# A retention layer and a snake MLP on one core: the second projection of blocks 1 to 8 as seven products of quarters, in a new order of all steps

## The chip, the cores and the metric

The kernel runs on one core of a Trainium2 chip. The metric is device time in microseconds (us), the median of several runs. Five engines work side by side, each through its own queue of instructions in order: TensorE (PE in the profile; its loads of weights are PEld), VectorE (DVE), ScalarE (ACT), GpSimd (POOL) and SyncE (SP, which issues DMAs here). Semaphores order them. PE writes its products to PSUM, which has 8 banks of 512 float32 per partition; GpSimd doesn't read PSUM in this kernel.

## The reference

A retention layer (attention with a decay in place of a softmax) for 8 batches of 576 positions and 8 heads of 64, and behind it an MLP with a snake activation, on 4608 tokens of 512 features:

```python
scores = scale * np.matmul(q, k.transpose(0, 1, 3, 2))
Dmat = np.where(rel >= 0, gamma[:, None, None] ** rel[None, :, :], 0.0)   # rel = pos[:, None] - pos[None, :]
attn_out = np.matmul(scores * Dmat[None, :, :, :], v)                      # per batch and head
x = attn_out.transpose(0, 2, 1, 3).reshape(4608, 512)
h = x @ w_in                                                               # 512 -> 2048
s = np.sin(alpha * h)
g = h + s * s / (alpha + 1e-09)
out = g @ w_out                                                            # 2048 -> 512
```

## The kernel before

The tokens fall into 9 blocks of 512: blocks 0 to 7 are the first 512 positions of a batch each, block 8 the last 64 positions of all eight. The program is one long table, `STEPS`: the order of the entries is the order in which the steps are issued, and with it the order on each engine; a letter behind a colon names the engine of a step (A ScalarE, V VectorE, G GpSimd, P TensorE, S SyncE), and `name=number` puts a tile into a numbered buffer or bank. A loop at the end of the kernel calls one function for each entry. Nothing else sets the order, and semaphores follow from who writes and reads which tile.

Attention of a batch `b`, in two halves `p` of 256 positions:

- `LD` loads raw q, k, v (SyncE), `CA` scales them to float16, `TU` and `TK` (PE and a copy) or `XP` (a DMA) turn q and k.
- `OU` makes the states k^T v of four chunks on PE; `TS` or `EV` copies them, `MA`, `MB` (or `NS`) and `ST` run the decay from chunk to chunk.
- `SC` makes the scores on PE, `MK` masks them on VectorE, `VA`, `VB` and `SA` add up values and states, and `KP` copies the result to the block's input `x`. `RL` is a mark that waits for `VA`, on GpSimd or another engine, or a drain of PE.
- Names with `E` (`LE`, `CE`, `XE`, `ESC` to `EKP`) do the same for the last 64 positions of the batches, block 8.

The MLP of block `n`, in 16 units `u` of 128 hidden features:

- `PR` (line 757) is the first projection of a unit: four products of 512 tokens into a bank; a few units go in two halves of 256 columns.
- `SI` (765) takes the sine on ScalarE, `SQ` (775, 776) squares it on ScalarE, VectorE or GpSimd, and `PD` (780) adds: g = sq * inva + h, on VectorE, and frees the bank.
- `G2.n.c.part` (796) is the second projection: for each of four chunks `c` of 128 tokens, 16 products of 512 output columns, in four parts; `FI` copies the bank to SBUF, `OS` (806, 807) stores it with two DMAs. The products of block n stand among the `PR` of block n + 1.

`KB` issues products of zeros on PE while it has nothing else to do. `WI` and `WO` load the two weights on GpSimd's queue, cast to float16. The file already has functions for a second projection by quarters (`TT`, `SM`, `PP`, `CP`, `AD`, `OQ`, lines 813 to 888); the table of before doesn't call them.

Of the kernel before, what the change touches and what calls it, by code (L numbers as in the profile page):

```python
# [23 lines left out]
CN; AR; EY; MC; Z0; ZE; FS; LD.0.k.0 raw.0.k.0=0; LD.0.q.0 raw.0.q.0=1; LD.0.v.0 raw.0.v.0=2; LD.0.q.1 raw.0.q.1=3  # L24
LD.0.k.1 raw.0.k.1=4; CA.0.k.0.0:G k16.0.0=0; LD.0.v.1 raw.0.v.1=5; CA.0.q.0.1:V q16.0.0=1; CA.0.k.0.1:V; CA.0.q.0.0:V
CA.0.v.0.2:A v16.0.0=2; LD.1.q.1 raw.1.q.1=6; KB.16.256.6; KB.44.64.6; OU.0.0 kv.0.0.0=0 kv.0.0.1=1
TU.0.k.0.0 tr.0.k.0=2; LD.1.q.0 raw.1.q.0=7; CA.0.q.1.2:G q16.0.1=3; TU.0.k.0.1; TU.0.q.0.0 tr.0.q.0=3
TK.0.k.0.0:V kT.0.0=4; TU.0.q.0.1; TS.0.0:V kvs.0=8; TK.0.k.0.1:A; CA.0.k.1.2:V k16.0.1=5; LD.1.v.0 raw.1.v.0=9
TK.0.q.0.2:A qT.0.0=6; WI.0; TU.0.q.1.2 tr.0.q.1=0; WI.2; TS.0.1:V; SC.0.0.1 sc.0.0.1=4; CA.0.v.1.2:V v16.0.1=7
TU.0.k.1.2 tr.0.k.1=1; LD.1.k.0 raw.1.k.0=10; MA.0.1:G s32.0.1=8; SC.0.0.0 sc.0.0.0=6; TK.0.k.1.2:A kT.0.1=9; MB.0.1:G  # L30
AT al=2; WI.1; ST.0.1:V s16.0=10; LD.1.k.1 raw.1.k.1=11; AC:A; TK.0.q.1.2:A qT.0.1=11; ST.0.0:V
CA.1.q.1.2:G q16.1.1=12 <ST.0.0; KB.10.256.3; OU.0.1 kv.0.1.0=0 kv.0.1.1=1; MA.0.2:G s32.0.2=13; TS.0.2:A
MK.0.0.1 ret.0.0.1=14; MB.0.2:G; WI.3; MK.0.0.0 ret.0.0.0=15; SC.0.1.0 sc.0.1.0=2; ST.0.2:G; TU.1.q.1.2 tr.1.q.1=0
WO.0; MK.0.1.0 ret.0.1.0=16; TK.1.q.1.2:A qT.1.1=17; SC.0.1.1 sc.0.1.1=4; LD.1.v.1 raw.1.v.1=12
CA.1.q.0.2:G q16.1.0=18; MK.0.1.1 ret.0.1.1=19; VA.0.0 o.0.0=6; RL.0.0:P; VB.0.0; SA.0.0; VA.0.1 o.0.1=2
KP.0.0.2:V x.0=13; RL.0.1:P; VB.0.1; SA.0.1; PR.0.2.0 hps.0.2=0; KP.0.1.0:V; KP.0.1.1:A; PR.0.2.1; PR.0.1.2 hps.0.1=2
SI.0.2 s.0.2=0; SQ.0.2:V ss.0.2=1; AI; SI.0.1 s.0.1=2; KB.2.512.6; PR.0.0.2 hps.0.0=3; PD.0.2 gT.0=0
LD.2.k.1 raw.2.k.1=14; SQ.0.1:A ss.0.1=3; NS.0.3; PR.0.8.0 hps.0.8=0; SI.0.0 s.0.0=4; PR.0.3.2 hps.0.3=4; PD.0.1
CA.1.v.0.2:A v16.1.0=20; SQ.0.0:V ss.0.0=5; PR.0.8.1; PD.0.0; SI.0.3 s.0.3=6; PR.0.11.2 hps.0.11=1; SI.0.8 s.0.8=7
SQ.0.3:G ss.0.3=8; TU.1.q.0.2 tr.1.q.0=5; PR.0.6.2 hps.0.6=2; TK.1.q.0.0:A qT.1.0=21; WO.1; PD.0.3; SI.0.11 s.0.11=9  # L40
LD.2.k.0 raw.2.k.0=15; PR.0.7.2 hps.0.7=3; TK.1.q.0.1:V; ST.0.3:G; SI.0.6 s.0.6=10; PR.0.5.2 hps.0.5=4; WO.2
SQ.0.11:A ss.0.11=11; SQ.0.6:V ss.0.6=12; SI.0.7 s.0.7=13; PD.0.6; PR.0.4.2 hps.0.4=5; LD.2.q.0 raw.2.q.0=0
SI.0.5 s.0.5=14; PD.0.11; SQ.0.7:G ss.0.7=15; PR.0.12.2 hps.0.12=2; SQ.0.8:A ss.0.8=0; SQ.0.5:V ss.0.5=1
SI.0.4 s.0.4=2; CA.1.k.0.2:G k16.1.0=22; PR.0.14.2 hps.0.14=1; PD.0.8; SI.0.12 s.0.12=3; PD.0.5; PR.0.9.0 hps.0.9=0
SI.0.14 s.0.14=4; PR.0.9.1; PD.0.7; SQ.0.14:A ss.0.14=5; SQ.0.12:G ss.0.12=6; LD.2.v.0 raw.2.v.0=1
TU.1.k.0.2 tr.1.k.0=4; PR.0.10.2 hps.0.10=3; PD.0.14; TK.1.k.0.2:A kT.1.0=23; PD.0.12; PR.0.15.0 hps.0.15=1
SI.0.9 s.0.9=8; PR.0.15.1; SQ.0.4:V ss.0.4=10; SI.0.10 s.0.10=9; PR.0.13.2 hps.0.13=2; SQ.0.9:V ss.0.9=12; PD.0.4
# [36 lines left out]
CA.4.k.0.2:G k16.4.0=19; SQ.2.2:A ss.2.2=4; G2.1.3.0 op.1.3=3; SQ.2.7:A ss.2.7=6; PD.2.2; G2.1.3.1; PD.2.7
# [130 lines left out]
def kernel(  # L215
# [10 lines left out]
    nc = tc.nc  # L226
# [4 lines left out]
    P = 128  # L231
# [77 lines left out]
    def halves(n):  # L309
        return slice(64 * n, 64 * n + 64)  # L310
# [631 lines left out]
```

## Time and profile before

| what | value |
|---|---|
| time, median of 3 runs | 311.0 us (309.82 to 311.75) |
| the profiled execution's own time | 310.68 us |
| its span, first to last instruction | 308.9 us |
| mean granted clock of TensorE | 0.991 |
| PE busy | 294.2 us (95%) |
| VectorE busy | 204.6 us (66%) |
| ScalarE busy | 181.4 us (59%) |
| GpSimd busy | 136.6 us (44%) |
| bytes moved by DMA | 49.84 MB, 161 GB/s on average |

A row of a group reads: line, engine, operation, what it writes and reads, shapes, count, then the time that all of them were busy and the mean of one in nanoseconds, then how long the engine stood idle right before them and for whom. A row of the order of time has the start, the length, the engine and the line, and the count where like instructions are merged. A row of a stretch has its bounds, its length and the busy time of each engine in the order PE, PEld, VectorE, ScalarE, GpSimd (or of one group alone), the granted clock, the busy share of the DMA engines and GB/s. Products overlap at their ends, so the length of one (379 ns) is more than the time from one to the next.

### The profile page before, as it was taken

To read this page: it belongs to the slowest core of one execution; us is meant where nothing else is said; L and a number is where in the kernel's file an instruction comes from. 1 tells how busy PE (TensorE), PEld (TensorE's weight loads), DVE (VectorE), ACT (ScalarE), POOL (GpSimd) and SP (SyncE) were. 2 spreads that over 40 slices of the span, in tenths; PEclk is the share of its full clock that TensorE was granted. 3 is DMA by queue.
4 is the path that set the end of the run, shared out by engine and by line. 5 is a ranking of instruction groups with operands and counts; after the bars stand their busy time and mean duration, and the time that the engine had idled before them with its cause. 6 is when DMAs were issued, how large, how long until landed. Compare 5 with 4: busy or idle time off the path is not lost.

```text
span 308.9 us, 7892 instructions
## 1 busy us (share of the span) xinstructions
PE 294.2 (95%) x3241; PEld 148.1 (48%) x3241; DVE 204.6 (66%) x297; ACT 181.4 (59%) x287; POOL 136.6 (44%) x154
## 2 busy tenths in 40 slices
PE   7769999999999999999999999899999999999994
PEld 5645556455444544454445444444454454444441
DVE  1587989899778786767666566766657745556500
ACT  1538946685356667675777577556764556555411
POOL 5794680299379497487168613970030000000000
PEclk9799999999999999999999999999999999999998
DMA  7999999997893978688797979774431111111232
GB/s 230 336 216 216 219 256 317 257 245 214 214 304 97 166 172 227 189 155 176 164 262 175 152 169 235 191 174 105 102 70 36 34 36 37 34 34 43 56 73 69
DMA packets 115380, 49.84 MB, mean 161 GB/s; under 512 B 69760, under 2 KB 110736, under 8 KB 115344
## 3 DMA queue, kind: packets, MB, share of 16 engines
q1 hardware_dynamic: 110912, 45.10, 61.3%
q0 software_dynamic: 4224, 4.19, 8.0%
q8 instruction: 25, 0.41, 0.6%
q10 hardware_dynamic: 208, 0.04, 0.1%
q14 instruction: 11, 0.09, 0.1%
HBM read 36.74 MB, written 9.44 MB: 149 GB/s over the span
## 4 chain that ended last, share of the span: by engine, by line
PE 64%; DMA 9%; POOL 8%; DVE 6%; SPq 5%; issue 4%; ACT 2%; POOLq 0%; ACTq 0%; DVEq 0%
PE banks L796 30%; PE banks L757 27%; DMA r<-in_q_dram 4%; POOL h L436 4%; SPq L409 3%; DVE g L780 2%; DMA r<-in_k_dram 2%; PE banks L539 2%; PE banks L570 2%; DMA r<-in_v_dram 2%; DMA s<-s 2%; DVE h L552 1%; DVE s L776 1%; POOL s L776 1%; ACT s L765 1%
## 5 line engine op out<-in xcount | busy, mean ns | idle before, releaser
L757 PE MATMUL banks<-r,w_in 128*128 128x512 f16 (+1 forms) x608 | 143.1, 368 | 1.1 <-DVE g L780 0.9
L796 PE MATMUL banks<-w_out,g 128*128 128x512 f16 x576 | 142.3, 379 | 0.1
L780 DVE SCALAR_TENSOR_TENSOR g<-s,inva,banks 128x512 f16<-128x512 f16 x144 | 106.2, 746 | 54.3 <-ACT s L775 46.1
L765 ACT ACTIVATE s<-banks,alpha 128x512 f16<-128x512 f32 x144 | 97.1, 687 | 71.3 <-PE banks L757 67.9
L757 PEld LDWEIGHTS <-w_in 128*128 128x128 f16 x608 | 58.4, 98 | 65.4 <-issue 1.6
L796 PEld LDWEIGHTS <-g 128*128 128x128 f16 x576 | 54.8, 98 | 65.0 <-issue 0.4
L436 POOL TENSOR_TENSOR h<-r,cn 128x1024 f16<-128x1024 f32 (+1 forms) x29 | 49.7, 1723 | 36.3 <-DMA r<-in_k_dram 24.2
L776 DVE TENSOR_TENSOR s<-s 128x512 f16<-128x512 f16 x72 | 40.3, 560 | 20.4 <-ACT s L765 18.0
L313 ACT COPY h<-banks 128x512 f32<-128x512 f32 (+2 forms) x41 | 25.9, 639 | 30.3 <-PE banks L796 21.5
L775 ACT ACTIVATE s<-s 128x512 f16<-128x512 f16 x62 | 38.8, 631 | 1.1
L552 DVE TENSOR_TENSOR h<-banks,mask 128x1024 f16<-128x1024 f32 (+1 forms) x32 | 35.2, 1119 | 2.5 <-PE banks L539 2.4
L313 ACT CAST r<-banks 128x1024 f16<-128x1024 f32 (+1 forms) x18 | 15.5, 873 | 8.3 <-PE banks L606 6.2
L644 POOL TENSOR_TENSOR s<-h,cn 128x512 f16<-128x512 f32 x8 | 8.7, 1087 | 23.1 <-PE banks L570 18.2
L515 POOL TENSOR_TENSOR r<-h,r 128x256 f32<-128x256 f32 x22 | 16.2, 735 | 3.2 <-ACT r L313 1.7
L313 POOL CAST h<-r 128x1024 f16<-128x1024 f32 (+1 forms) x10 | 10.1, 1016 | 14.2 <-DMA r<-in_v_dram 14.1
L776 POOL TENSOR_TENSOR s<-s 128x512 f16<-128x512 f16 x10 | 10.3, 1037 | 12.5 <-ACT s L765 12.5
L436 DVE TENSOR_TENSOR h<-r,cn 128x512 f16<-128x512 f32 (+1 forms) x11 | 10.9, 1031 | 5.3 <-DMA r<-in_q_dram 5.3
L512 POOL TENSOR_TENSOR h<-r,cn 128x256 f32<-128x256 f32 x22 | 14.3, 650 | 0.2
L570 PE MATMUL banks<-h 64*64 64x128 f16 (+1 forms) x512 | 11.0, 214 | 2.9 <-POOLq L587 1.1
L526 POOL TENSOR_TENSOR h<-r,cn 128x256 f16<-128x256 f32 x19 | 12.8, 676 | 0.8 <-ACT r L313 0.2
L539 PE MATMUL banks<-h 64*64 64x128 f16 (+1 forms) x512 | 11.1, 218 | 0.8 <-ACT r L313 0.5
L539 PEld LDWEIGHTS <-h 64*64 64x64 f16 x512 | 7.8, 108 | 7.9 <-issue 6.7
(48 smaller groups left out, 107.3 us busy)
## 6 DMA issues: line engine op xcount, KB each, us to landing
out_dram<-h SPq DMA_DIRECT2D x72, 128.0 KB, 2.5
r<-in_q_dram SPq DMA_DIRECT2D x16, 512.0 KB, 6.0
r<-in_k_dram SPq DMA_DIRECT2D x10, 512.0 KB, 13.6
r<-in_v_dram SPq DMA_DIRECT2D x10, 512.0 KB, 6.0
r<-in_k_dram SPq DMA_DIRECT2D x24, 128.0 KB, 3.2
r<-in_v_dram SPq DMA_DIRECT2D x24, 128.0 KB, 3.3
w_in<-in_moe_w_in_dram POOLq DMA_DIRECT2D x4, 512.0 KB, 11.7
w_out<-in_moe_w_out_dram POOLq DMA_DIRECT2D x4, 512.0 KB, 11.0
```

What stands on the lines that cost most here:

```text
L313: return eng.copy(d_, s_) if eng is nc.scalar else eng.tensor_copy(d_, s_)
L436: return eng.tensor_tensor(dst[:, a0:a1].rearrange("p a r t d -> p t (a r) d"), t_.rearrange("p (t a) x -> p t a x", t=2)[:, :, a0:a1].rea ...
L515: return eng.tensor_tensor(sum_of(b, c), s32(b, c), sum_of(b, c), ADD)
L539: i = matmul(sc[halves(g), t, c : c + n], kT[halves(t), 2 * a + r, halves(g)], qT[halves(t), 2 * a : 2 * a + 2, 64 * g + i0 : 64 * g + 64] ...
L552: return nc.vector.tensor_tensor(ret(b, p, y).rearrange("p t (z x) -> p (t z) x", z=2)[:, :, 0:n], bank(f"sc.{b}.{p}.{y}", 2).rearrange("p ...
L570: made.append(matmul(o[halves(e), t, c : c + 128].rearrange("p (r i) -> p r i", r=2)[:, :, i0:64], v16[halves(g), 4 * t + 2 * x + e, r, :] ...
L757: i = matmul(bank(hps)[:, cols], w_in16[:, a, u * P : (u + 1) * P], x_of(n)[:, a, cols], start=starts(hps), stop=(a == KT - 1), skip_group ...
L765: return nc.scalar.activation(small(f"s.{name}")[:, cols], bank(f"hps.{name}")[:, cols], mybir.ActivationFunctionType.Sin, bias=0.0, scale ...
L775: return nc.scalar.activation(ss_t, s_t, mybir.ActivationFunctionType.Square)
L776: return eng.tensor_tensor(ss_t, s_t, s_t, MULT)
L780: return nc.vector.scalar_tensor_tensor(g_of(n)[:, u, cols], small(f"ss.{name}")[:, cols], inva[:, u : u + 1], bank(f"hps.{name}")[:, cols ...
L796: i = matmul(bank(f"op.{n}.{c}"), g_of(n)[:, fk, c * P : (c + 1) * P], w_out16[:, fk, :], start=starts(f"op.{n}.{c}"), stop=True, skip_gro ...
```

## The change

Blocks 1 to 8 replace `G2`, `FI` and `OS` (64 products of 512 columns, four copies of 128x512, eight output DMAs per block) by a product of quarters. The block's 512 tokens, the 2048 hidden features and the 512 output columns are each cut in two, so that g is A11, A12, A21, A22 (256 tokens x 1024 features) and `w_out` is B11, B12, B21, B22 (1024 x 256). Seven products of quarters then do what eight would do in the plain form (the scheme of Winograd):

- `TT` (once): T1 = B12 - B11, T2 = B22 - T1, T3 = B22 - B12 and T4 = B21 - T2, each in two steps of 128x1024 half-precision elements; all eight on VectorE.
- `SM` (each block): S1 = A21 + A22, S2 = S1 - A11, S3 = A11 - A21 and S4 = A12 - S2, each in two steps of 128x1024; 39 on VectorE, 25 on GpSimd. S1 and S4 are written over quarters of g.
- `PP.n.p.j` on PE: product p in four steps of four products of 256 columns (16 per product, 112 per block). P1, P6, P7 and P4 go into one bank, X, and add up there; P2 goes to Y, P5 and P3 to Z.
- `CP` copies a bank (P2; U2 = P1 + P6; U3 = U2 + P7; C21 = U3 + P4), 24 on ScalarE and 8 on VectorE; `AD` on VectorE adds a bank to such a copy: C11 = P1 + P2, C22 = P5 + U3, C12 = P5 + P3 + U2.
- `OQ` stores a quarter of the output (256 tokens x 256 columns) with two DMAs; rows are 1 KB, not 2 KB.

Block 0 keeps `G2`. The functions, which stand in the file before and after alike:

```python
def SM(n, s, i, eng):
    i *= 4
    S = {x: of_units(big16(f"S{x}.{n}"), i, 4) for x in (2, 3) if f"S{x}.{n}" in place}
    S[1], S[4] = quarter_a(n, 1, 0, i, 4), quarter_a(n, 0, 1, i, 4)
    a, b, op = {
        1: lambda: (S[1], quarter_a(n, 1, 1, i, 4), ADD),
        2: lambda: (S[1], quarter_a(n, 0, 0, i, 4), SUB),
        3: lambda: (quarter_a(n, 0, 0, i, 4), S[1], SUB),
        4: lambda: (S[4], S[2], SUB),
    }[s]()
    return eng.tensor_tensor(S[s], a, b, op)

BANK_OF = {1: "X", 6: "X", 7: "X", 4: "X", 2: "Y", 5: "Z", 3: "Z"}

def PP(n, p, j):
    ps = bank(f"{BANK_OF[p]}.{n}")
...
    for u in us:
...
        for c in cs:
            i = matmul(
                ps[:, 256 * c : 256 * c + 256], left[:, 0, 128 * c : 128 * c + 128], right[:, 0, :],
                start=starts(f"{BANK_OF[p]}.{n}"), stop=True, skip_group_check=True,
            )
    return i

KEPT = {2: ("Y", "p2"), 6: ("X", "u2"), 7: ("X", "u3"), 4: ("X", "c21")}

def CP(n, p, eng):
    b, t = KEPT[p]
    return copy(eng, mid32(f"{t}.{n}"), bank(f"{b}.{n}"))

SUMS = {11: ("X", "p2"), 22: ("Z", "u3"), 12: ("Z", "u2")}

def AD(n, c, h=2):
    b, t = SUMS[c]
    cols = slice(0, 512) if h == 2 else slice(256 * h, 256 * h + 256)
    x = mid32(f"{t}.{n}")[:, cols]
    return nc.vector.tensor_tensor(x, bank(f"{b}.{n}")[:, cols], x, ADD)
```

The rest of the change is the table. Every step has a new place, and many have a new engine: squares go from 62 on ScalarE, 72 on VectorE and 10 on GpSimd to 81, 24 and 39; of the sums `MA` and `MB`, 44 on GpSimd before, 17 go to VectorE. The dummies `KB` stand in 14 entries instead of 4, all but one ahead of the first `PR`, and are 72 products before and after. Lines move by 17. In the diff, two lines of the table (the end of block 8 in both) and the one line of code:

```diff
-G2.8.3.0 op.8.3=1; FI.8.2:A osb.8.2=22; G2.8.3.1; OS.8.2; G2.8.3.2; G2.8.3.3; FI.8.3:A osb.8.3=6; OS.8.3
+PP.8.5.2; PP.8.4.0; AD.8.22; PP.8.4.3; PP.8.4.2; OQ.8.22; PP.8.4.1; PP.8.3.1; CP.8.4:A c21.8=25; PP.8.3.2; OQ.8.21
+PP.8.3.3; PP.8.3.0; AD.8.12.1; AD.8.12.0; OQ.8.12.1; OQ.8.12.0
...
-        return (nc.scalar if h == 1 else eng).dma_start(x[1][:, cs], t[halves(1), cs])
+        return (nc.scalar if h < 2 else eng).dma_start(x[1][:, cs], t[halves(1), cs])
```

The places that the prediction speaks of, as rows of the engines' queues, stand there. In those rows the tiles go by their pools: r is a buffer of the 16 of float32 (raw inputs, states, the sums T and S), h one of the 28 of float16, s the small ones of the sine and the square, g the hidden layer, banks PSUM.

More of the change, by code (lines that the diff above doesn't have):

```diff
@@ new lines @@
+PR.0.6.2 hps.0.6=5; SI.0.4 s.0.4=11; ST.0.3:G; PD.0.8; PR.0.5.2 hps.0.5=7; SQ.0.4:G ss.0.4=12; SI.0.6 s.0.6=13
+PD.0.11; LD.2.k.1 raw.2.k.1=14; SI.0.9 s.0.9=14; PR.0.15.0 hps.0.15=3; CA.1.v.0.2:G v16.1.0=22; PD.0.4
+PR.0.12.2 hps.0.12=6; SI.0.5 s.0.5=15; SQ.0.3:A ss.0.3=0; SQ.0.5:V ss.0.5=2; WO.3; PR.0.14.2 hps.0.14=2
+SQ.0.6:A ss.0.6=4; PD.0.3; SQ.0.9:G ss.0.9=3; SI.0.7 s.0.7=5; PD.0.5; PR.0.10.2 hps.0.10=4; SI.0.14 s.0.14=1
+SQ.0.7:V ss.0.7=6; PR.0.15.1; SQ.0.14:G ss.0.14=7; PD.0.7; SI.0.10 s.0.10=10; G2.0.1.0 op.0.1=7; PD.0.6
@@ new lines @@
+PD.7.8; PP.6.3.2; PP.7.1.1; AD.6.12; PP.6.4.0; SM.7.3.0:V S3.7=12; PP.7.1.0; OQ.6.12; CP.6.4:V c21.6=21; EVA.1 oe.1=2
+EVA.0 oe.0=6; PR.7.7.2 hps.7.7=0; ERL.1:A; ERL.0:G; OQ.5.21; EVB.0; SI.7.7 s.7.7=14; ESA.1; EVB.1; ESA.0
+EKP.1.0:V x.8=11; PR.7.9.2 hps.7.9=1; EKP.0.0:A; OQ.3.12; SQ.7.7:V ss.7.7=0; EKP.1.1:V; PR.7.10.2 hps.7.10=5
+SI.7.9 s.7.9=13; EKP.0.1:A; PR.7.14.2 hps.7.14=2; SQ.7.9:G ss.7.9=10; PR.7.13.2 hps.7.13=3; SI.7.14 s.7.14=8; PD.7.9
+SI.7.10 s.7.10=15; PR.7.12.2 hps.7.12=6; PD.7.7; SI.7.13 s.7.13=3; SQ.7.10:G ss.7.10=7; PP.7.2.0 Y.7=7
```

378 lines of the change are left out of this document (192 added, 186 removed).

## Prediction

> **What bounds the kernel now.** I read the page first, then the groups by form, then the order of time at the end, then stretches.
>
> The page, engines and chain of waits:
>
> ```profile
> PE 294.2 (95%) x3241; PEld 148.1 (48%) x3241; DVE 204.6 (66%) x297; ACT 181.4 (59%) x287; POOL 136.6 (44%) x154
> PE 64%; DMA 9%; POOL 8%; DVE 6%; SPq 5%; issue 4%; ACT 2%; POOLq 0%; ACTq 0%; DVEq 0%
> ```
>
> A busy PE need not be at its peak, so I look for its pace. Groups by form (busy us, mean ns of one, idle before them and releasers), then the order of time from the last run of products to the end (start, length):
>
> ```profile
> L796 PE MATMUL banks<-w_out,g 128*128 128x512 f16 x576 | 142.3, 379 | 0.1
> L780 DVE SCALAR_TENSOR_TENSOR g<-s,inva,banks 128x512 f16<-128x512 f16 x144 | 106.2, 746 | 54.3 <-ACT s L775 46.1 <-POOL s L776 3.9
> ...
> 289.61 14.84 PE L796 MATMUL banks<-w_out,g 128*128 128x512 f16 x68
> ...
> 304.49 0.58 ACT L313 COPY h<-banks 128x512 f32<-128x512 f32 x1 [2.87 <-PE banks L796]
> 305.10 0.47 SPq L806 DMA_DIRECT2D out_dram<-h  x1
> 305.61 0.60 SPq L807 DMA_DIRECT2D out_dram<-h  x1
> ```
>
> 68 products in 14.84 us, the last of 0.379: (14.84 - 0.379) / 67 = 0.2158 us from start to start. The 576 of the second projection wait 0.1 us in all. Vector (DVE) idles 54 us for its sums `PD` (L780) while PE idles for nobody: PE sets the time from its first projection to the last product, and the copy, two issues and landing behind that take 4.5 us. Only fewer or shorter products help, as long as the other engines keep up.
>
> **The products.** Blocks 1 to 8 drop 8 x 64 = 512 products of 512 columns and get 8 x 7 x 16 = 896 of 256. The pace of the short form is in the trace, in halved first projections (order of time, PE and its weight loads):
>
> ```profile
> 50.12 1.04 PE L757 MATMUL banks<-r,w_in 128*128 128x256 f16 x8
> ...
> 50.12 0.97 PEld L757 LDWEIGHTS <-w_in 128*128 128x128 f16 x9
> ```
>
> A single one lasts 0.273 us in the row of its form below, so (1.04 - 0.273) / 7 = 0.1096 us each, with a load of 128x128 weights beside every one. Removed: 512 x 0.2158 = 110.5 us. Added: 896 x 0.1096 = 98.2 us. **Net -12.3 us**, all on the path. The first projections keep their number and halves, attention its products.
>
> The Trainium skill, "TensorE: Matmul & The Clock Gate", Part 3, The mechanism, says that a weight load overlaps running matmuls only when it goes to another row group. The trace does not agree: these loads use all rows and lie inside the 0.1096 us. It is a rival below.
>
> **Vector's new work.** Rows of the forms that price it:
>
> ```profile
> L776 DVE TENSOR_TENSOR s<-s 128x512 f16<-128x512 f16 x72 | 40.3, 560 | 20.4 <-ACT s L765 18.0 <-DMA s<-s 1.6
> L757 PE MATMUL banks<-r,w_in 128*128 128x256 f16 x64 | 8.6, 272 | 0.6 <-DVE g L780 0.4 <-DVE r L313 0.2
> L436 DVE TENSOR_TENSOR h<-r,cn 128x512 f16<-128x512 f32 x8 | 7.1, 923 | 5.3 <-DMA r<-in_q_dram 5.3
> L436 DVE TENSOR_TENSOR h<-r,cn 128x1024 f16<-128x1024 f32 x3 | 3.9, 1319 | 0.0
> L313 DVE COPY h<-banks 128x512 f32<-128x512 f32 x2 | 1.4, 680 | 0.0
> L313 DVE COPY r<-banks 128x256 f32<-128x256 f32 x2 | 0.8, 413 | 0.0
> L776 POOL TENSOR_TENSOR s<-s 128x512 f16<-128x512 f16 x10 | 10.3, 1037 | 12.5 <-ACT s L765 12.5
> L436 POOL TENSOR_TENSOR h<-r,cn 128x1024 f16<-128x1024 f32 x21 | 40.7, 1945 | 35.4 <-DMA r<-in_k_dram 23.2 <-DMA r<-in_q_dram 12.0
> L515 POOL TENSOR_TENSOR r<-h,r 128x256 f32<-128x256 f32 x22 | 16.2, 735 | 3.2 <-ACT r L313 1.7
> L512 POOL TENSOR_TENSOR h<-r,cn 128x256 f32<-128x256 f32 x22 | 14.3, 650 | 0.2
> L775 ACT ACTIVATE s<-s 128x512 f16<-128x512 f16 x62 | 38.8, 631 | 1.1
> L313 ACT COPY h<-banks 128x512 f32<-128x512 f32 x34 | 19.8, 586 | 24.7 <-PE banks L796 21.5 <-DMA out_dram<-h 2.9
> ...
> 240.00:300.00 60.00, 8.88 (x21) 1.00 0.18 43
> ```
>
> The last row is a stretch view of L776 alone on Vector: 8.88 / 21 = 0.42 us for 512 half-precision elements while GpSimd (POOL) is idle. The two copies from PSUM give 0.267 us for 256 further elements and 0.147 fixed. So 512 in 0.42 is twice the rate of the copies, and a sum `SM` or `TT` of 1024 elements comes to 0.147 + 2 x (0.42 - 0.147) = 0.69 us. This form is not in the trace. Its ends are 0.42 (as cheap as half its size) and 1.32 (the 1024 row of L436); I take 0.70, nearest to the row with the same operation and types. `AD` has one operand in PSUM and one in SBUF like `PD`: 0.75.
>
> Vector over the program: squares 72 to 24, -20.2; `SM` 39 x 0.70 = +27.3; `TT` 8 x 0.70 = +5.6; `AD` 23 x 0.75 and 2 halves, +18.0; `CP` 8 x 0.68 = +5.4; `MA` and `MB` 17 x 0.42 (256 elements, as the second copy) = +7.1; the steps that change places with other engines (`EV` +4, `CE` +3, `EKP` +2, `KP` +1 and so on) about +7. Sum +50: 204.6 becomes some 255 us of about 297. ScalarE (ACT): squares +19 x 0.63 = 12, copies of results 34 to 27 at 0.59, -4, `CA` some +5, others -4: 181 to some 190. GpSimd: squares +29 x 1.04 = 30, `SM` 25 at an estimated 2.07 (twice the 512 row) = 52, 8 `MA`, 9 `MB`, 4 `CA` and 5 `CE` less, -24: 137 to some 195. None reaches PE over the whole program, but a stage can.
>
> The place is the end of block 0 to the start of block 2, where `TT` is made. Vector's rows of before there (squares and sums of block 1, and the scaling of q and k, L436):
>
> ```order
> L436 TENSOR_TENSOR h_68<-r_67,cn 128x2x4x64 x2
> L526 TENSOR_TENSOR sS<-r_67,cn 128x256
> L436 TENSOR_TENSOR h_68<-r_67,cn 128x2x8x64 x2
> L776 TENSOR_TENSOR s_69<-s_69 128x512
> L313 COPY h_68<-banks 128x512
> L780 SCALAR_TENSOR_TENSOR g_70<-s_69,inva,banks 128x512
> ```
>
> and now (17 lines lower; L849 is `TT`, L453 `CA`, L793 squares, L797 `PD`):
>
> ```order
> L849 TENSOR_TENSOR r_67<-w_out_65 128x1024
> L453 TENSOR_TENSOR h_68<-r_67,cn 128x2x8x64
> L849 TENSOR_TENSOR r_67<-w_out_65 128x1024
> L849 TENSOR_TENSOR r_67<-w_out_65,r_67 128x1024 x3
> L453 TENSOR_TENSOR h_68<-r_67,cn 128x2x8x64 x2
> L793 TENSOR_TENSOR s_69<-s_69 128x512
> L330 COPY h_68<-banks 128x512
> L797 SCALAR_TENSOR_TENSOR g_70<-s_69,inva,banks 128x512 x2
> ```
>
> Five of the eight `TT` stand ahead of block 1's first `PD`, and each `PD` behind them frees a bank that PE waits to fill. The stretch from `PR.0.14` to `PR.2.3`, by its times in before:
>
> ```profile
> 32.50:76.80 44.30, 43.39 (x634) 23.97 (x633) 41.05 (x60) 29.00 (x48) 27.88 (x29) 1.00 1.09 255
> ```
>
> PE, its loads, Vector, ACT, POOL: PE is busy 43.4 of 44.3 us, Vector 41.05. In the same stretch of the new table PE has 3 wholes of `G2` and 3 halves of `PR` less, 8 quarters of products and one `OU` more: -2.6 - 1.3 + 3.5 + 0.85, so 44.7. Vector has `TT` 5.6, 2 `SM` 1.4, 2 `PD` 1.5, `MA` and `MB` 1.3 more, 4 squares 1.7, and copies and `CA` some 2.8 less: +5.3, so 46.3. If Vector never waits, PE loses 46.3 - 44.7 = 1.6 us; if it waits as it does now (3.25 us), 4.9. I take **+3**.
>
> Elsewhere Vector also meets GpSimd. L776 on Vector, stretches with GpSimd at work:
>
> ```profile
> 60.00:100.00 40.00, 3.92 (x7) 1.00 0.86 217
> 100.00:140.00 40.00, 6.10 (x10) 1.00 0.84 181
> 140.00:180.00 40.00, 7.12 (x10) 1.00 0.87 189
> ```
>
> 0.56, 0.61 and 0.71 us in place of 0.42: 0.14 to 0.29 more for one, 0.2 as their middle. Operations of Vector with two SBUF inputs go from 93 to 111, and GpSimd, which they meet, from 137 to 195 us. 111 x 0.2 less the 93 x 0.14 that 204.6 holds (0.560 - 0.42 for a square on average) is +9: Vector 264 us, still under PE. I take **+1** for the stages where it binds briefly, between 0 and 5.
>
> The Trainium skill, "SBUF — State Buffer", SBUF: two separate sides, says that Vector with two SBUF inputs and GpSimd lock a shared port pair for a whole instruction, and the loser blocks. The trace agrees (0.42 alone, 0.71 beside GpSimd). By the rule `PD` and `AD`, with one operand in PSUM, would not block.
>
> **The head.** First products wait for `w_in`, issued by GpSimd (order of time; first product):
>
> ```profile
> 11.37 1.68 POOL L383 DMA_DIRECT2D w_in<-in_moe_w_in_dram  x2
> ...
> 14.76 0.80 POOL L383 DMA_DIRECT2D w_in<-in_moe_w_in_dram  x1
> ...
> 21.42 2.06 PE L757 MATMUL banks<-r,w_in 128*128 128x256 f16 x12 [0.19 <-DVE r L313]
> ...
> DMA to landing us min/median/max: 8.5/11.7/12.4
> ```
>
> GpSimd's rows in the head, before (L383 is `WI`, L512/L515 `MA`/`MB`):
>
> ```order
> L436 TENSOR_TENSOR h_68<-r_67,cn 128x2x8x64
> L383 DMA w_in_64<-in_moe_w_in_dram 128x4x512 x2
> L512 TENSOR_TENSOR h_68<-r_67,cn 128x256
> L515 TENSOR_TENSOR r_67<-h_68,r_67 128x256
> L383 DMA w_in_64<-in_moe_w_in_dram 128x4x512
> ```
>
> and now (L400 is `WI`, L543 `ST`):
>
> ```order
> L453 TENSOR_TENSOR h_68<-r_67,cn 128x2x8x64
> L400 DMA w_in_64<-in_moe_w_in_dram 128x4x512 x2
> L453 TENSOR_TENSOR h_68<-r_67,cn 128x2x8x64
> L543 TENSOR_TENSOR h_68<-r_67,cn 128x256
> L529 TENSOR_TENSOR h_68<-r_67,cn 128x256
> L400 DMA w_in_64<-in_moe_w_in_dram 128x4x512
> ```
>
> The third load (units 4 to 7) now also stands behind `RL.0.1`, a mark on GpSimd that waits for `VA.0.1` on PE; `WI.3`, `WO` and block 1's scaling queue behind it. From `VA.0.1` to `PR.0.4`, its first user, PE has some 8.5 us of work (4 wholes and 6 halves of `PR` 6.1, ten dummies 1.1, attention and a transposition 1.3), and the load takes 8.5 to 12.4: PE waits 0 to 4 us. Against that v of block 0 is loaded fifth, not third, so q and k come sooner, by up to 2 us. The 72 dummies `KB` stay 72, but none is below 256 columns now where 44 were of 64: +4 us (8.4 for 4.5 by 0.11 per 256 columns) if waits don't hide them; they stand where PE waits for `TK` and `MK`. I take 0, between -2 and +6.
>
> **Hand-overs, loads, tail.** P1, P6, P7 and P4 share bank X, with `AD` or `CP` between; a hand-over takes 0.9 us (the last short product 0.27, the 0.04 from 304.45 to 304.49 above, the copy 0.59), and the order puts other products of at least 0.87 behind it: nothing, at most 2 us in all. SP issues 74 output DMAs for 72, loads stand earlier, rows are 1 KB: hidden, as DMA is at 0.18 in the last 60 us. The last copy becomes half an `AD` (0.41 for 0.58): nothing.
>
> **Sum.** The profiled execution took 310.68 (span 308.9), 0.3 under the median 311.0. 308.9 - 12.3 + 3 + 1 = 300.6 span, 302.4 for the execution, **302.7** against the median.
>
> **Rivals.** (1) All arrives: Vector catches up behind its stretch, as it has 45 us to spare in all: 298.7. (2) The head is late: `w_in` 4 us, dummies 1 to 2: 308. For: DMA is full there (1.09 in the stretch from 32.5 us). Against: the earlier q and k. (3) Vector becomes the bound: 255 less 13 of lock is 242; the 47 sums at 1.32, +29, and 64 others 0.29 more each, +19: 290, of which 11 in the head. With Vector at work 0.95 of the time, 279 / 0.95 + 21.4 + 4.5 = 320 span, **322**; it decides once Vector needs more than some 280 us. For: it is at work 0.93 of the stretch above already. Against: squares on Vector run at twice the rate. (4) Weight loads not hidden, by the skill's rule above: 384 more at 0.098 us, +37.6, 349. Against: the row at 50.12.
>
> **How the numbers follow.** Forecast 0.41 (300 to 306), (1) 0.25 (297 to 300), (2) 0.20 (305 to 311), (3) 0.13 (311 to 322), (4) 0.01. A measurement here tells about 1% from no change: 307.9 and 314.1. Faster: 0.41 + 0.25 + half of (2) = 0.76; same: the other half and a quarter of (3) = 0.13; slower 0.11. The range 297 to 312 leaves out most of (3), (4) and a little of (1).
>
> **What would show it.** Right: the short products 0.109 us apart; the first projection of block 0 starting near 21 us; PE's waits for Vector's `g` a few us, in 35 to 80 us; Vector near 255 to 265 busy. Wrong: `SM` over 1 us on Vector, PE waiting for `g` or for the sums in every block, or a wait for `w_in` around 27 us.

## The result, and the profile after

| | before | after |
|---|---|---|
| time, median of 11 runs each | 312.02 us (309.82 to 313.15) | 307.48 us (304.0 to 309.55) |
| ratio, 95% interval | | 0.984 (0.981 to 0.988) |
| the profiled execution, its span | 310.68, 308.9 us | 308.33, 306.6 us |
| PE, VectorE, ScalarE, GpSimd busy | 294.2, 204.6, 181.4, 136.6 us | 291.2, 244.6, 188.5, 200.1 us |

Medians and ranges, here and below, are of all executions; ratios and their intervals leave out single executions that took over 1.5% longer than the fastest of the same kernel.

The change makes the kernel 1.6% faster, 4.5 us where 9.3 were forecast against a median of 312.0 (8.3 against the 311.0 that was known then). 307.5 lies within the range of 297 to 312, but outside the 300 to 306 of the forecast itself. So the question is where the other half went.

The page of after: engines, the granted clock in 40 slices of 7.7 us, and the shares of the chain of waits.

```profile
PE 291.2 (95%) x3625; PEld 187.0 (61%) x3625; DVE 244.6 (80%) x353; ACT 188.5 (61%) x301; POOL 200.1 (65%) x181
PEclk9999999999999999997899999999999999999999
PE 66%; DVE 12%; DMA 7%; ACT 4%; SPq 4%; issue 3%; POOL 3%; DVEq 0%; ACTq 0%; POOLq 0%
```

PE still sets the time. New is the dip of the clock at 138 to 153 us (before had one in its second slice). The groups by form, for the prices that the prediction had to estimate:

```profile
L880 PE MATMUL banks<-w_out,g 128*128 128x256 f16 x384 | 51.7, 276 | 0.1
L861 DVE TENSOR_TENSOR r<-g 128x1024 f16<-128x1024 f16 x20 | 16.2, 818 | 0.2
L861 DVE TENSOR_TENSOR g<-g 128x1024 f16<-128x1024 f16 x10 | 7.3, 726 | 0.5 <-POOL r L861 0.3
L861 POOL TENSOR_TENSOR r<-g 128x1024 f16<-128x1024 f16 x12 | 26.0, 2172 | 7.0 <-DVE g L797 6.1 <-DVE g L861 0.8
L898 DVE TENSOR_TENSOR h<-banks,h 128x512 f32<-128x512 f32 x23 | 15.6, 684 | 7.1 <-PE banks L880 5.7 <-ACT h L330 1.4
...
151.98 1.91 PE L880 MATMUL banks<-r 128*128 128x256 f16 x16
```

A sum of 1024 elements (`SM`, L861) costs Vector 0.73 to 0.82 us and GpSimd 2.17 in these rows, an `AD` (L898) 0.68, close to the estimates of 0.70, 2.07 and 0.75. A short product (L880) lasts 0.276 us on average and its group waits 0.1 us in all; in the run of 16 in the last row, products start (1.91 - 0.273) / 15 = 0.109 us apart, as the prediction said.

The longest waits of PE among those of the program's work, and PE's order of time around 140 us:

```profile
PE banks L556 <- DMA h<-h: 3.6, 1, 3.6
PE banks L774 <- DVE h L330: 1.0, 1, 1.0
...
138.52 0.42 PE L587 MATMUL banks<-h 64*64 64x128 f16 x16
142.57 0.53 PE L556 MATMUL banks<-h 64*64 64x128 f16 x16 [3.64 <-DMA h<-h]
...
145.89 1.91 PE L880 MATMUL banks<-w_out,g 128*128 128x256 f16 x8
```

PE stands for 3.64 us ahead of the scores of block 5, for a transposed k that a DMA writes. Behind it, eight short products take 1.91 us, where eight of 256 columns took 1.04 in the prediction's row: they run at about half the pace. What SP issued ahead of that transpose (L426 `LD`, L651 `LE`, L904 and L905 `OQ`, L485 `XP`):

```profile
129.95 0.61 SPq L905 DMA_DIRECT2D out_dram<-h  x1
130.67 2.69 SPq L426 DMA_DIRECT2D r<-in_v_dram  x4
133.47 1.28 SPq L485 DMA_TRANSPOSE h<-h  x1
134.80 0.61 SPq L651 DMA_DIRECT2D h<-in_q_dram  x1
135.46 0.63 SPq L651 DMA_DIRECT2D h<-in_k_dram  x1
136.13 1.19 SPq L651 DMA_DIRECT2D h<-in_q_dram  x1
138.43 2.60 SPq L485 DMA_TRANSPOSE h<-h  x2
```

and, from the chain of waits in order of time, its end:

```profile
138.60 1.08 SPq L485
...
139.78 2.75 DMA h<-h
```

SP has no pause but one of about 1 us at 137.4, where `XP.5.k.1` waits for its buffer 3, which `XP.5.q.0` (133.47) still reads: it goes out at 138.43, 5.0 us behind `XP.5.q.0`. The three loads `LE` between the two fit into this wait and do not lengthen it. `XP.5.k.0`, for which PE stands, is the last of the three; it goes out at 139.78 and lands 2.75 us later. A stretch view shows what follows (PE, its loads, Vector, ACT, POOL, then clock, DMA share, GB/s):

```profile
140.00:150.00 10.00, 7.33 (x70) 4.10 (x71) 2.18 (x4) 2.33 (x3) 2.68 (x2) 0.66 0.76 179
```

A clock of 0.66 on average over 10 us is half the clock for 6.8 us: another 3.4 us lost. The trace's record of the clock agrees: 0.5 for 6.83 us. Wait and clock together are 7 us at one place.

### The profile page after: what moved, and what is told of

It reads as the page before. It is cut to its first block, busy times and chain, and to the rows that moved or that the text cites. A ratio compares the mean times of both kernels' runs of the same rounds, so it can differ in the third digit from the quotient of the medians.

```text
span 306.6 us, 8737 instructions
## 1 busy us (share of the span) xinstructions
PE 291.2 (95%) x3625; PEld 187.0 (61%) x3625; DVE 244.6 (80%) x353; ACT 188.5 (61%) x301; POOL 200.1 (65%) x181
## 4 chain that ended last, share of the span: by engine, by line
PE 66%; DVE 12%; DMA 7%; ACT 4%; SPq 4%; issue 3%; POOL 3%; DVEq 0%; ACTq 0%; POOLq 0%
PE banks L880 28%; PE banks L774 28%; DVE g L797 6%; DMA r<-in_q_dram 4%; SPq L430 3%; PE banks L813 3%; ACT s L782 2%; PE banks L556 2%; DVE s L793 2%; PE banks L587 2%; DMA s<-s 2%; PE banks L504 1%; ACT s L792 1%; PE banks L623 1%; POOL s L793 1%
## 5 line engine op out<-in xcount | busy, mean ns | idle before, releaser
L880 PEld LDWEIGHTS <-g 128*128 128x128 f16 x640 | 61.9, 98 | 19.6 <-issue 1.5
L793 POOL TENSOR_TENSOR s<-s 128x512 f16<-128x512 f16 x39 | 42.0, 1082 | 40.9 <-ACT s L782 37.8
L880 PE MATMUL banks<-w_out,g 128*128 128x256 f16 x384 | 51.7, 276 | 0.1
L569 DVE TENSOR_TENSOR h<-banks,mask 128x1024 f16<-128x1024 f32 (+1 forms) x32 | 35.4, 1115 | 5.2 <-PE banks L556 4.6
L880 PE MATMUL banks<-r,g 128*128 128x256 f16 x256 | 35.2, 273 | 0.1
L861 POOL TENSOR_TENSOR r<-g 128x1024 f16<-128x1024 f16 x12 | 26.0, 2172 | 7.0 <-DVE g L797 6.1
L880 PEld LDWEIGHTS <-r 128*128 128x128 f16 x256 | 24.8, 98 | 6.4 <-issue 0.3
L898 DVE TENSOR_TENSOR h<-banks,h 128x512 f32<-128x512 f32 (+1 forms) x25 | 16.4, 663 | 9.9 <-PE banks L880 8.5
L861 POOL TENSOR_TENSOR g<-g,r 128x1024 f16<-128x1024 f16 x7 | 15.6, 2232 | 10.7 <-PE banks L880 9.9
L793 DVE TENSOR_TENSOR s<-s 128x512 f16<-128x512 f16 x24 | 16.6, 692 | 5.8 <-ACT s L782 5.8
L880 PE MATMUL banks<-w_out,r 128*128 128x256 f16 x128 | 16.9, 273 | 0.0
L861 DVE TENSOR_TENSOR r<-g 128x1024 f16<-128x1024 f16 x20 | 16.2, 818 | 0.2
```

Of the source, the lines that this page charges most:

```text
L569: return nc.vector.tensor_tensor(ret(b, p, y).rearrange("p t (z x) -> p (t z) x", z=2)[:, :, 0:n], bank(f"sc.{b}.{p}.{y}", 2).rearrange("p ...
L793: return eng.tensor_tensor(ss_t, s_t, s_t, MULT)
L861: return eng.tensor_tensor(S[s], a, b, op)
L880: i = matmul(ps[:, 256 * c : 256 * c + 256], left[:, 0, 128 * c : 128 * c + 128], right[:, 0, :], start=starts(f"{BANK_OF[p]}.{n}"), stop= ...
L898: return nc.vector.tensor_tensor(x, bank(f"{b}.{n}")[:, cols], x, ADD)
```

## The experiments

Two theories stood at the start. **A**: the products gained what was forecast, and SP's queue, which makes block 5's transposes late, takes it back. **B**: Vector or GpSimd, with 104 us more work between them, hold PE up.

### The changed kernel again

No edit.

> The changed kernel once more, nothing edited. Theory A (the transposes of block 5's k come late because SP's queue issues without a pause from about 93 us on; that is a property of the order): the wait of TensorE on h<-h near 139 us is there again, 3 to 4.5 us long, and the time is 305 to 309 us, 0.980 to 0.990 of the kernel before. Rival B (the 3.64 us were an accident of one execution): no wait of TensorE on a DMA over 1 us there, and a time near 303 us.

307.5 us, ratio 0.982 (0.977 to 0.987). The wait is there, 3.88 us at the same place, and the half clock behind it too:

```profile
143.21 0.53 PE L556 MATMUL banks<-h 64*64 64x128 f16 x16 [3.88 <-DMA h<-h]
...
140.00:150.00 10.00, 6.70 (x67) 3.78 (x68) 2.23 (x4) 2.33 (x3) 2.69 (x2) 0.66 0.82 177
```

It is no accident of one execution, but single runs go down to 304.3, so it isn't in each of them at its full price.

### Block 5's transposes earlier

```diff
 CP.2.4:A c21.2=6;
+XP.5.k.0 kT.5.0=3;
 LE.3.q;
 ...
-XP.5.k.1 kT.5.1=3
 ...
-XP.5.k.0 kT.5.0=13
 ...
+XP.5.k.1 kT.5.1=13
 OS.0.1
```

> The two transposes of block 5's k stand earlier in SP's order: XP.5.k.0 ahead of the block 3 q load for the last stage (LE.3.q), XP.5.k.1 ahead of OS.0.1. Nothing else is edited. Theory A: the 3.64 us wait and the half clock after it (together the 6.8 us lost in the stage from PR.3.3 to PR.4.1) go; 301 to 304 us, 0.968 to 0.976 of the kernel before, loss of that stage 0 to 2 us. Rival B (Vector is late at that place anyway, and the wait only stands where another would): the stage still loses 5 us or more, TensorE waits for DVE or ACT there, and the time stays at 306 to 309 us.

The edit also lets the two change places and buffers: `XP.5.k.0` now goes first and writes buffer 3. The profile did as A says. The stretch from `PR.3.3` to `PR.4.1`, of after and of this run, by its own times in each (the clock is the third figure from the end):

```profile
107.88:147.60 39.72, 35.90 (x435) 23.39 (x433) 30.34 (x44) 25.96 (x42) 26.00 (x20) 0.93 0.93 188
```

```profile
108.13:142.25 34.12, 33.43 (x434) 22.18 (x432) 30.26 (x43) 25.18 (x41) 24.89 (x20) 1.00 0.91 183
```

The same work takes 5.6 us less; that execution took 303.3 us, next to the forecast of 302.7. The median fell only to 305.55 (303.3 to 308.2), with a ratio of 0.981 (0.976 to 0.985) that overlaps the one above. So the mechanism is shown in the profile and its size on the median is not: the other executions of this kernel have granted clocks of 0.984 to 0.999, so some probably still wait; that is not shown, since one execution of each kernel is profiled. The next transpose still writes buffer 3, which `XP.5.q.0` reads. Here it goes out 3.5 us behind `XP.5.q.0`; in the profile of the run without the sums of w_out below, where these transposes stand in the same places, 4.9 us behind it, and there PE waits 2.23 us again.

### The loads for the last stage on ACT's queue

With the transposes early, all 24 `LE` are issued by ACT:

```diff
-LE.7.k rs.3.k=10
+LE.7.k:A rs.3.k=10
```

> The order of the run with the early transposes, with the 24 loads for the last stage (LE, 16 us of issuing on SP) issued by ACT in their old places in the order. Theory A (SP's queue, which issues for 16 to 19 of each 20 us until 200 us, still makes transposes late in some executions, and this is what keeps the median 2 us above the profile): 302 to 304.5 us, and the highest run under 306. Rival B (ACT is next: 24 issues of about 0.5 us and their waits for buffers stand ahead of its sines): 306 to 309 us, TensorE waits for ACT s or DVE g. Rival C (the spread is the granted clock's, not a queue's): 305 to 306 us, spread as before.

303.36 us (302.45 to 304.3), ratio 0.975 (0.972 to 0.977), the clock 0.998 to 1.0 in every execution. A's time came: with 24 issues less on SP, neither the wait nor the dip shows. SP's load as such is not new, though: it issues 180 plain DMAs and 32 transposes in the kernel before and in the changed one, which take 208 and 211 us in their profiles; what is new is the order. With these loads on ACT `XP.5.q.0` goes out at 132.26 us, where it went out at 133.17 with them on SP; how this keeps every execution fast is not shown further. Two runs tell whether the gain belongs to the new order. The kernel before with the same edit:

> The kernel before, with its 24 loads for the last stage (LE) issued by ACT in their old places, nothing else. Theory A (it is the new order that makes TensorE wait for what SP issues; the page of the kernel before has no wait of TensorE on a DMA): 310 to 313 us, ratio 0.995 to 1.005. Rival B (a freer SP queue helps any order, so the gain of this edit says nothing of the change): 307 to 309.5 us, ratio under 0.992.

313.34 us, ratio 1.005 (1.002 to 1.008): no gain, so the old order did not suffer from these loads on SP. And the changed kernel with its transposes in their old places:

> The changed kernel with its transposes in their old places, and its 24 loads for the last stage (LE) issued by ACT. Theory A (the transposes of block 5's k are late by what stands ahead of them on SP, three of these loads among it): the 3.6 to 4.0 us wait near 139 us falls under 2 us, no half clock behind it, 303 to 305.5 us. Rival B (only the place of the transposes in the order counts, SP's other work does not): wait and half clock stay, 306 to 308 us.

306.27 us, from 302.6 to 310.0, ratio 0.977 (0.971 to 0.983). Here rival B was right about the wait: the profiled execution, which is the slowest of the six (310.0), still has it, while the fastest, at a clock of 1.0, took 302.6. PE's wait, and SP's row of the three transposes:

```profile
PE banks L557 <- DMA h<-h: 3.1, 1, 3.1
...
133.39 8.48 SPq L486 DMA_TRANSPOSE h<-h  x3
```

No load stands between the three any more, and still the second goes out only at 139.21, 5.8 us behind the first, for which it waits. So the loads between the transposes were not what held them up: the buffer that two of them share was, and the time the first takes to land. Taking load off SP is not enough alone; the place of the transposes counts too.

### Only one more transpose moved

On top of the early transposes (loads on SP again), `XP.5.q.0` ahead of `LD.6.v.1`:

```diff
 CA.5.q.0.2:G q16.5.0=3;
+XP.5.q.0 qT.5.0=26;
 LD.6.v.1 raw.6.v.1=6;
 ...
-XP.5.q.0 qT.5.0=26;
```

> The order with the early transposes (305.55 us, 303.3 to 308.2, loads for the last stage on SP), with one step more moved: XP.5.q.0 ahead of the four loads LD.6.v.1 on SP. XP.5.q.0 reads buffer 3, and the transpose of block 5's k behind it writes buffer 3, so that one waits on SP until the first has landed (issue at 133.2 to 133.4 us, the next at 136.7 to 138.3 in the runs so far). Theory A (this chain of two transposes through one buffer, and not SP's load as such, is what comes late in some executions): both transposes come 1 to 2.5 us earlier, no half clock, 303 to 304.5 us with under 3 us between lowest and highest. Rival B (SP's load as such): 305 to 306.5 us, spread as before. Rival C (XP.5.q.0 itself now waits on SP, for the outputs that leave buffer 26, and holds up the loads behind it): a new wait of TensorE for a load near 140 to 150 us, 306 us or more.

304.19 us, ratio 0.974 (0.970 to 0.978), the clock 0.996 or more in every execution as A expects, but the runs go from 302.7 to 307.2 as B expects. The move did less than it was meant to: in the profiled execution (307.2 us) `XP.5.q.0` goes out at 132.53 us and `XP.5.k.0` behind it at 136.67, where they went out at 133.17 and 136.69 without the move. There several waits of 0.6 to 1.1 us stand spread from 134 us on, for GpSimd, Vector and the transpose. So this chain is one cause of the late runs and not all of them; what else varies from run to run stays open.

### The second projection plain, in the new order

In the order with the early transposes, 64 products of 512 columns a block stand in the 28 places of the 112 short ones; `SM`, `TT` and `AD` are gone, and the four results are copied out where a bank was kept or summed:

```diff
-PP.4.1.0 X.4=3
+GU.4.1.0.1 op.4.1=3
 ...
-CP.4.7:A u3.4=27
+FI.4.1:A osb.4.1=27
 ...
-OQ.4.22
+OS.4.1
```

`GU.n.c` with a list of units makes their products of chunk `c`.

> The order of the run with the early transposes (305.55 us), but blocks 1 to 8 make their second projection by plain products again: 64 products of 512 columns a block in the 28 places of the 112 short ones, in three banks as before, each quarter of the rows copied out where a kept or summed bank was; the sums TT, SM and AD are left out since nothing reads them. Nothing is left out of the result. Theory A (the products give about 12.3 us and the sums lie beside TensorE's work outside of the first 80 us): 8 to 13 us more, 313 to 318 us. Rival B (the sums on Vector and GpSimd cost nearly what the products save): 304 to 308 us. Rival C (the new order is itself worse or better than the old one): under 309 us it is better, over 319 us worse.

316.18 us (315.36 to 316.32), ratio 1.015 (1.013 to 1.017). Engines of that profile:

```profile
PE 301.1 (96%) x3241; PEld 148.6 (47%) x3241; DVE 196.8 (63%) x285; ACT 185.7 (59%) x297; POOL 140.4 (45%) x156
```

This splits the change in two. Products with their sums, in the same order: 305.55 - 316.18 = **-10.6 us**. The order, with plain products: 316.18 - 311.56 = **+4.6 us**. Both figures hold for this pair of runs, with the transposes early: the plain products stand in places laid out for short ones, so the order alone may cost less, and the late transposes of the changed kernel are not in it.

### The sums left out or moved

Without the sums of w_out's quarters:

> The order of the run with the early transposes, with the eight sums of w_out's quarters (TT, 5.8 us of Vector between 49 and 73 us) left out; the products that read them read quarters of w_out in their place, so the values are not the reference's and the products' count and shapes stay. Theory A (the stretch from PR.0.14 to PR.2.3 is Vector's, and these sums are its price): the 1.2 us wait near 58 us goes, the loss of the stage PR.1.4 to PR.2.3 falls from 2.7 us to 1 us or less, and the time falls by 1.5 to 3 us, to 302.5 to 304 us. Rival B (TensorE is bounded there by the chain from gate to gate whatever Vector does): loss and time stay within 0.5 us.

304.73 us, ratio 0.979 (0.976 to 0.981): 0.8 us less by the medians. The stretch from `PR.1.4` to `PR.2.3`, after the early transposes, then without `TT`:

```profile
47.93:81.51 33.58, 32.05 (x477) 18.10 (x476) 32.35 (x47) 23.79 (x39) 22.16 (x20) 1.00 1.01 236
```

```profile
48.13:81.24 33.11, 31.89 (x478) 18.05 (x477) 27.30 (x39) 23.79 (x39) 21.24 (x20) 1.00 1.01 241
```

Vector has 5 us less to do and PE gains 0.5 (0.65 up to 133 us, by the starts of the same products in both profiles; behind it the wait for the transpose sets this profile back). Theory A had 1.5 to 3. The 1 us wait at 58 us is still there; Vector's rows of after just ahead of it say why:

```profile
56.68 1.85 DVE L793 TENSOR_TENSOR s<-s 128x512 f16<-128x512 f16 x1 [0.49 <-ACT s L782]
58.46 0.68 DVE L330 COPY h<-banks 128x512 f32<-128x512 f32 x1
```

```profile
56.35 3.08 POOL L453 TENSOR_TENSOR h<-r,cn 128x1024 f16<-128x1024 f32 x2 [7.78 <-DMA r<-in_q_dram]
```

A square that takes 0.42 us alone takes 1.85 beside GpSimd's scaling, and the copy that frees PE's bank (`FI.0.1`) stands behind it. Without any sum:

> As the run without the sums of w_out's quarters, and all 64 sums of gates (SM) left out as well, and each of the 24 additions of a bank into a kept sum (AD) cut to 8 of 512 columns; the products read gates in place of sums. Vector is relieved by some 50 us and GpSimd by 54. Theory A (all sums behind the first 80 us are hidden): within 1 us of the run without the sums of w_out's quarters. Rival B (Vector or GpSimd holds TensorE up in the blocks, a bit at a time): 3 us or more under it, below 300 us. Rival C (the two engines' lock makes Vector's other work slow): Vector's mean SQ and CA fall by 20% or more.

305.05 us, ratio 0.980 (0.976 to 0.984): Vector is busy for 197.3 us in place of 245.6 and GpSimd for 138.9 in place of 200.8, with almost no gain on the median. Rival B falls. Of rival C something is there (a square on Vector takes 0.60 us on average in place of 0.73, 18% less), but it buys little time. The median hides a part: by the starts of the same products, this profile is 1.0 us ahead of the one with all sums up to 133 us, then loses 5.1 to waits and half clock up to 159 us, and gains 1.1 behind that. So all sums together cost an estimated 2 us. The other way round, GpSimd's 25 sums on Vector:

```diff
-SM.1.3.0:G
+SM.1.3.0:V
```

> All 25 sums of units (SM) that GpSimd makes at 2.17 us each are made by Vector, at about 0.73 us each: GpSimd's busy time falls by about 54 us to 146, Vector's rises by about 18 us to 263. Theory A (TensorE and SP's queue set the time, Vector has 60 us to spare outside of the first 80 us): 306 to 311 us, within 1% of the changed kernel. Rival B (Vector is near to being the bound in the blocks): each added 0.73 us is paid, and the time rises by 10 to 18 us, to 317 to 325 us.

312.04 us, ratio 1.000 (0.998 to 1.002), about 5 us over the changed kernel. Neither theory's time:

```profile
PE 291.5 (94%) x3625; PEld 186.8 (60%) x3625; DVE 261.4 (84%) x378; ACT 188.3 (61%) x301; POOL 147.0 (47%) x156
...
PE banks L880 <- DVE h L898: 3.8, 3, 2.7
PE banks L774 <- DVE g L797: 3.1, 5, 1.5
```

PE now waits for `AD` and `PD`, and no longer for the transpose. Vector's price is therefore more than the 5 us: the product that starts at 122.89 us in the changed kernel starts at 130.80 here, 7.9 us later. 6.6 of it come back up to 150 us, because PE now arrives behind the transposes; after that 3.7 are lost again. So 17 us more on Vector cost an estimated 11.6 us where Vector decides, which is nearer to rival B than the time shows. At 245 us Vector costs little, at 261 a lot, long before it is full.

### The sums of w_out later

`TT.2` stands ahead of `SM.1.2.1`, `TT.4` ahead of `PP.1.7.3`:

```diff
-TT.2.0:V T2=8; PR.1.5.1; PR.1.6.2 hps.1.6=5; TT.2.1:V; LD.4.k.0 raw.4.k.0=9; TT.4.1:V T4=10
+PR.1.5.1; PR.1.6.2 hps.1.6=5; LD.4.k.0 raw.4.k.0=9
 ...
+TT.2.0:V T2=8; TT.2.1:V; SM.1.2.1:V
 ...
+TT.4.1:V T4=10; TT.4.0:V; PP.1.7.3
```

> The sums of w_out's quarters that are not needed first (TT.2.0, TT.2.1, TT.4.0, TT.4.1, each about 0.7 us on Vector) stand later in Vector's order: TT.2 ahead of SM.1.2.1, TT.4 ahead of PP.1.7.3, in place of among block 1's gates. Theory A (the predicted 3 us of the stretch from PR.0.14 to PR.2.3 are the price of these sums on a Vector that is full there): the wait of 1.1 us at 57.8 us goes and the loss of the stage PR.1.4 to PR.2.3 falls from 2.6 to 1.5 us or less; the time falls by about 1 us, 306 to 307 us. Rival B (PE had slack there, or Vector's other work fills the gap): loss of the stage stays 2 to 3 us, time unchanged.

311.98 us, ratio 0.994 (0.991 to 0.998): some 4 us slower than the changed kernel, which neither theory held. Vector, GpSimd and PE at the new place of `TT.4` (L849):

```profile
88.86 4.36 DVE L849 TENSOR_TENSOR r<-w_out,r 128x1024 f16<-128x1024 f16 x2
...
88.24 2.13 POOL L861 TENSOR_TENSOR g<-g,r 128x1024 f16<-128x1024 f16 x1
90.32 3.80 POOL L453 TENSOR_TENSOR h<-r,cn 128x1024 f16<-128x1024 f32 x2
...
94.41 0.42 PE L556 MATMUL banks<-h 64*64 64x128 f16 x16 [2.92 <-DVE h L569]
...
90.00:100.00 10.00, 6.37 (x63) 4.21 (x62) 9.96 (x11) 2.51 (x5) 5.12 (x4) 0.83 0.64 169
```

Two sums that take 1.36 us at their old place take 4.36 beside GpSimd's, the masks (L569) come late, PE waits 2.92 us, and 3.4 us at half clock follow. At 100 us PE is 6.5 us behind the changed kernel; 4.6 of it come back at the transposes, where the wait shrinks to 1.8 us and no half clock follows. This execution took 308.9 us, hardly more than the changed kernel's 308.3, so what makes the median 312 is not shown by it.

### All mends together

To the early transposes and the loads on ACT, five steps moved, for four waits:

```diff
+FI.0.1:V osb.0.1=12; CA.2.q.0.2:V    (from behind SI.1.5)
+KP.3.0.2:A x.3=14; LE.7.k:A          (LE.3.k:A behind SI.2.15, LE.0.v:A behind EV.7.1)
+XE.1.k kTe.1=15; OQ.1.21             (from behind VA.7.0)
```

> The order with the early transposes and the loads on ACT (303.36 us), with four more moves of one step each, each aimed at one wait of TensorE in that run: FI.0.1 ahead of CA.2.q.0 on Vector (1.07 us at 57.8 us, where a square that Vector shares time with GpSimd for took 1.74 us ahead of the copy), LE.7.k and LE.3.k behind KP.3.0.2 and SI.2.15 on ACT (1.28 us at 105), LE.0.v behind EV.7.1 (0.83 us at 196), XE.1.k ahead of OQ.1.21 on SP (1.14 us at 229). Theory A (TensorE is the bound and each wait is paid in full): 3 to 4 us less, 299.5 to 301 us. Rival B (other work is late at the same places, the waits come back a little later): 301.5 to 304 us.

301.75 us (300.92 to 303.87), ratio 0.969 (0.965 to 0.973): 1.6 us under the version before it, within rival B's range at its lower end, and the fastest of all, 9.9 us under the kernel before. Of the 4.3 us that the four waits had, two gains stayed in the profile (0.8 us at 197 us, 1.2 at 231); of the 1.3 at 106 us most was lost again by 118, and of the 1.1 at 59 most within 1 us, to waits for Vector, as B had it. The longest wait that its profile names is the 1.3 us at the start for the zeros of the dummies, which all these kernels have. The next by their sums (in all, how many, the longest):

```profile
PE banks L774 <- DVE g L797: 1.2, 3, 0.5
PE banks L556 <- DVE g L797: 0.5, 1, 0.5
```

## Why the prediction was right, and where it was wrong

- **The products, -12.3.** Right. In one order, plain against short, the spans are 314.4 and 301.6 us, both at a clock of 1.00: 12.8, with the price of the sums in it. On the medians 10.6. The short products start 0.109 us apart with a weight load each, so the loads are hidden and rival 4 is out. (Its 349 is a slip: 37.6 on top of the forecast's 302.7 gives 340.)
- **Vector and GpSimd busy, about 255 (264) and 195.** 244.6 and 200.1. Rival 3 (Vector becomes the bound) did not come, but less room was left than "45 us to spare": 17 us more cost an estimated 11.6 where Vector decides, and 5 on the median.
- **The stretch of Vector, +3.** The size is near what the stretch lost, the cause does not fit. From `PR.1.4` to `PR.2.3` stand 84 products of 512 columns (0.2158 us each), 64 of 256 (0.1096) and attention's small ones (5.7 us by their pace): PE's work is 30.8 us, and the stretch of after took 33.43: 2.6 lost. But leaving out `TT` gave back 0.5 of it there and 0.8 us of the time, and with plain products and no sums at all the same place lost 2.3. The prediction added Vector's work up over the stretch; the one long wait of PE there, 1.0 us, was for one copy behind one square that GpSimd held up. Where the rest of the 2.6 us goes is not shown.
- **The other stages, +1.** Near. Without all sums the median falls by 0.5 us, and the profile gives an estimated 2 us for all of them, `TT` with its 0.65 among them. The forecast gave 4.
- **The head, 0.** Right: the first projection of block 0 starts at 20.76 us (21.42 before), and the wait for `w_in` behind it, at 28.0 us, is 0.18. Rival 2 is out. Yet 307.5 lies in the 305 to 311 of rival 2 and not in the forecast's own 300 to 306: that the time fell into the whole range is in part luck.
- **Hand-overs, loads, tail: "hidden".** This is the step that failed. It counted output DMAs (74 for 72, of which SP issues 72 as before and ACT two) and looked at the share of the DMA engines in the last 60 us. It did not look at SP's queue as a place where instructions stand in line, nor at which transposes stand last in it and share a buffer. The late transpose cost 7 us in the profiled execution, wait and half clock together; the early transposes with the loads on ACT took 4.1 us off the median (307.5 to 303.4).
- **The sum.** 302.7 was forecast. With the transposes early the profiled execution took 303.3, with the loads on ACT the median is 303.4. Part of that agreement is luck: the forecast gave the sums 4 us, the runs give them 0.5 to 2 and the new order, with what is left of its small waits, up to 4.6.

## What to carry to other kernels

When an order is rewritten, follow every queue that the bound engine waits for, SP's too: list what stands ahead of each transfer that is needed soon, and which buffer makes one transfer wait for another to land. The number of DMAs and the DMA engines' share do not tell: SP issues as many in both kernels here. A change that shows no effect, or a small one, can have moved a wait from one place to another; compare the starts of the same products. And price a wait of the bound engine at more than its length, and ask of each Vector operation with two SBUF inputs what GpSimd does at that moment, before asking how busy Vector is on average.

## What the runs showed of the hardware that was not expected

**The clock after a wait.** The mean clock over the 10 us around or behind a wait of PE:

| run | wait of PE | clock over 10 us |
|---|---|---|
| changed kernel, two profiles | 3.64, 3.88 us | 0.66, 0.66 |
| its loads on ACT, transposes in their old places | 3.12 us | 0.66 |
| sums of w_out later | 2.92 us, and 0.7 behind it | 0.83 |
| GpSimd's sums on Vector | 2.70 us | 0.83 |
| without sums of w_out | 2.23 us | 0.83 |
| without any sums | 1.06 and 0.99 us, 1.4 us apart | 0.83 |
| sums of w_out later, at the transposes | 1.78 us | 1.00 |
| one more transpose moved | 1.1 and 1.0 us, 6 us apart | 1.00 |
| early transposes; loads on ACT; all mends | none over 1 us from 140 to 150 us | 1.00 |

0.66 is 6.8 us at half clock, 0.83 is 3.4: steps of 3.4 us, each of which costs 1.7 again. (The clock's record in the traces has 6.83 and 3.41 us at 0.5.) The Trainium skill, "TensorE: Matmul & The Clock Gate", Part 1, What's actually happening, says that the clock halves after an idle window of about 3.4 us, with windows that run freely. The steps agree; the waits that sufficed here, 2.2 us or two of 1 us close together, are shorter than such a window, and a single one of 1.78 us did not suffice.

**Vector beside GpSimd.** A sum of 1024 half-precision elements went from 0.68 to 2.2 us on average (4.36 for two), a square from 0.42 to 1.85. The Trainium skill, "SBUF — State Buffer", SBUF: two separate sides, has the loser of the shared ports block for the whole instruction, which agrees: these ended 0.3 to 0.55 us behind the GpSimd operation beside them. `PD`, which reads PSUM, stayed at 0.741 us on average over all 144.

**Transposes on SP.** A DMA transpose holds SP's queue for 1.28 us where a plain load takes 0.63, and one that overwrites the buffer which the transpose before it reads waits there for that one: it went out 3.5 to 5.8 us behind it in these profiles. From issue to landing, transposes of this kind took 2.8 us in the kernel before and 3.8 in the changed one (medians).
